# Rows of ordered experts in two blocks of 112 partitions, bounds two less, the second part's rows turned later, the last rows weighted by two engines

## The chip, the core and the metric

The kernel runs on one core of a Trainium2 chip. The metric is the device time of one launch in microseconds (us). The kernel before takes 459.31 us, the median of three runs (458.78 to 460.84). The profile is one execution of the same program under the hardware profiler; its span is 464.4 us. The engines are TensorE (PE; its weight loads are listed apart as PEld), VectorE (DVE), ScalarE (ACT), GpSimd (POOL) and SyncE (SP), which issues most transfers. Sixteen DMA engines move the data.

## The reference

A gated linear attention is followed by a mixture of experts in two levels. Only the second half is touched here; it reads the attention's output as `x` of 3072 rows by 384.

```python
g_idx = argmax(x @ w_group, axis=1)            # 4 groups
g_w   = softmax(x @ w_group)[rows, g_idx]
out = zeros((3072, 384))
for g in range(4):
    mask_g = g_idx == g
    xg = x[mask_g]
    e_idx = argmax(xg @ w_expert[g], axis=1)   # 4 experts in each group
    e_w   = softmax(xg @ w_expert[g])[rows, e_idx]
    for e in range(4):
        mask_e = e_idx == e
        h  = maximum(xg[mask_e] @ w1[g, e], 0) # 384 -> 1024
        ye = h @ w2[g, e]                      # 1024 -> 384
        out[rows of g, e] = (g_w * e_w)[:, None] * ye
```

So each of 3072 rows goes to one of 16 experts. With these inputs the experts get between 158 and 213 rows. One expert's two matrices are 3 MB.

## The kernel before

The attention sends each finished row, with its weight and its row number (386 floats in all), by an indirect transfer into the slots of its expert in DRAM (`slots_d`). Then 17 jobs follow. Jobs 0 and 1 do expert 0: 128 early rows, and 96 more slots. Jobs 2 to 16 do the other 15 experts in order of their number of rows. The order is known only at run time, so a job of rank `r` has a fixed bound `cap(r)` of slots: 220, 218, 214, 212 and so on down to 178. A slot without a row holds zeros and a row number that is out of bounds, so that it is not written. Rows beyond the bound would be done by a loop at the end, once for each 128 of them.

```python
def cap(r):
    return CAP - 4 - 3 * r + r % 2            # CAP = 224
...
jobs = [dict(e=e, parts=[(0, EARLY)], rows=early_rows[:, e:e + 1, :]) for e in range(FIXED)]
jobs += [dict(e=e, parts=[(0, CAP - EARLY)]) for e in range(FIXED)]
jobs += [dict(r=r, parts=[(0, cap(r) // 2), (cap(r) // 2, cap(r) // 2)]) for r in range(NS)]
```

A job's rows are fetched into two parts of equal size. Part 0 holds the even slots and part 1 the odd slots, so that a partition takes two neighbouring slots of 1544 B each, 3088 B in one piece:

```python
def fetch_rows(job):
    e, (_, n), k = expert(job), job["parts"][0], len(job["parts"])
    job["rows"] = mp.tile([P, 2, XW], F32, name="xg", bufs=5)
    c0 = EARLY if k == 1 else 0
    nc.sync.dma_start(
        out=job["rows"][0:n, 0:k, :],
        in_=slots_d.rearrange("(e n) w -> e n w", e=NE)[ds(e, 1), c0:c0 + k * n, :].rearrange(
            "o (p t) w -> (o p) t w", t=k))
```

For each job, `columns` turns the rows (`xt`, by TensorE), `hidden` makes `hT` (line 628 on TensorE, line 630 on ScalarE), `result` makes `yT` (lines 643 and 645), and `deliver` turns it back, weights it, and scatters the rows to the output. `deliver` for a job runs inside the next job's `hidden`.

```python
def deliver(yT, c0, n, weight, dst):
    zy = bank()                                            # one of 7 PSUM banks
    for dc in range(DC):
        nc.tensor.transpose(zy[0:n, dc * P:(dc + 1) * P], yT[:, dc, c0:c0 + n], ident)
    yo = mp.tile([P, DM], F32, name="yo", bufs=3)
    nc.vector.tensor_scalar(out=yo[0:n], in0=zy[0:n, 0:DM], scalar1=weight, ...)   # L657
    nc.gpsimd.indirect_dma_start(out=out_by.popleft(), out_offset=dst, in_=yo[0:n], ...)  # L659
...
for j, job in enumerate(jobs):
    if 1 < j < len(jobs) - AHEAD:
        fetch_rows(jobs[j + AHEAD])                        # AHEAD = 3
    e, (_, n), k = job["e"], job["parts"][0], len(job["parts"])
    w1, w2 = weights[max(0, j - 1)]
    dst = mp.tile([P, 2], I32, name="dst")                 # two buffers
    nc.vector.tensor_copy(out=dst[0:n, 0:k], in_=job["rows"][0:n, :k, DM + 1])     # L805
    hT = hidden(w1, xt, k * n, {2: [deliver_last], 4: [last_gates] if j == 0 else []})
    if j == 0:
        order, excess, ceiling = by_number()
        fetch_rows(jobs[1])
        load_weights(1, expert(jobs[2]))
        for ahead in jobs[2:AHEAD + 2]:
            fetch_rows(ahead)
    elif j + 2 < len(jobs):
        load_weights(j + 1, expert(jobs[j + 2]))           # two buffers of w1, two of w2
    if j + 1 < len(jobs):
        xt = columns(jobs[j + 1], *([nc.scalar.copy] if j == 0 else []))   # turns, L613
    ...
    last = (job, result(w2, hT, k * n), dst)
deliver_last()
```

[...]

Of the kernel before, what the change touches and what calls it, by code (L numbers as in the profile page):

```python
# [16 lines left out]
ALU = mybir.AluOpType  # L17
AF = mybir.ActivationFunctionType
# [16 lines left out]
def gla_then_hierarchical_moe(  # L35
# [32 lines left out]
    nc = tc.nc  # L68
# [10 lines left out]
    DM = H * D  # L79
# [8 lines left out]
    CAP = 224  # L88
    FIXED, EARLY, EARLY_T = 1, P, (B - 1) * NC
    NS = NE - FIXED  # L90

    def cap(r):
        return CAP - 4 - 3 * r + r % 2

    NX = -(-(N - CAP) // P)
    XW = DM + 2
# [8 lines left out]
    def bank():  # L105
        return pp.tile([P, 512], F32, name="bank")
# [58 lines left out]
    def load_weights(i, e):  # L165
        w1 = wp.tile([P, DC, F], F32, name="w1")
        w2 = wp.tile([P, FC, DM], F32, name="w2")
        nc.sync.dma_start(out=w1.rearrange("p c f -> p (c f)"),
                          in_=w1_d[ds(e, 1)].rearrange("o p f -> p (o f)"))
        nc.sync.dma_start(out=w2.rearrange("p c f -> p (c f)"),  # L170
                          in_=w2_d[ds(e, 1)].rearrange("o p f -> p (o f)"))
        weights[i] = (w1, w2)
# [20 lines left out]
    with ExitStack() as gla:  # L193
# [17 lines left out]
        for u in range(3):  # L211
            w = units[u][2] * (2 * P + A1) + 1
            for p in range(HP):
                if not spare or width + w > DC * F:
                    k = len(spare)
# [333 lines left out]
        for n in range(LAST):  # L549
# [47 lines left out]
            if n == 2:  # L597
                nc.sync.dma_start(
                    out=slots_d.rearrange("(e n) w -> e n w", e=NE)[:, 0:CAP, :].rearrange(
                        "e (p t) w -> p e (t w)", t=2),  # L600
                    in_=blank[0:CAP // 2, None, :].to_broadcast([CAP // 2, NE, 2 * XW]))
# [7 lines left out]
    def turned(xg, xt, n, c0, copy=nc.vector.tensor_copy):  # L609

        z = bank()
        for dc in range(DC):
            nc.tensor.transpose(z[:, dc * P:dc * P + n], xg[0:n, dc * P:(dc + 1) * P],  # L613
                                ident[0:n, 0:n])
        copy(  # L615
            out=xt[:, :, c0:c0 + n],
            in_=z[:, 0:DM].rearrange("p (c t) -> p c t", c=DC)[:, :, 0:n])

    def hidden(w1, xt, n, between={}):
        hT = mp.tile([P, FC, CAP], F32, name="hT")  # L620
        for f0 in range(0, FC, 2):
            for fn in between.get(f0, ()):
                fn()
            z = bank()
            for k in range(2):
                f = f0 + k
                for dc in range(DC):
                    nc.tensor.matmul(z[:, k * n:(k + 1) * n], lhsT=w1[:, dc, f * P:(f + 1) * P],  # L628
                                     rhs=xt[:, dc, 0:n], start=(dc == 0), stop=(dc == DC - 1))
            nc.scalar.activation(out=hT[:, f0:f0 + 2, 0:n],  # L630
                                 in_=z[:, 0:2 * n].rearrange("p (f t) -> p f t", f=2), func=AF.Relu)
        return hT

    def result(w2, hT, n):

        yT = mp.tile([P, DC, CAP], F32, name="yT")
        for d0 in range(0, DC, 2):
            k = min(2, DC - d0)
            z = bank()
            for i in range(k):  # L640
                dc = d0 + i
                for f in range(FC):
                    nc.tensor.matmul(z[:, i * n:(i + 1) * n], lhsT=w2[:, f, dc * P:(dc + 1) * P],  # L643
                                     rhs=hT[:, f, 0:n], start=(f == 0), stop=(f == FC - 1))
            nc.scalar.copy(out=yT[:, d0:d0 + k, 0:n],  # L645
                           in_=z[:, 0:k * n].rearrange("p (c t) -> p c t", c=k))
        return yT

    out_by = deque(dram_disjoint_views(out, 2 * NE + 1))

    def deliver(yT, c0, n, weight, dst):

        zy = bank()
        for dc in range(DC):
            nc.tensor.transpose(zy[0:n, dc * P:(dc + 1) * P], yT[:, dc, c0:c0 + n], ident)  # L655
        yo = mp.tile([P, DM], F32, name="yo", bufs=3)
        nc.vector.tensor_scalar(out=yo[0:n], in0=zy[0:n, 0:DM], scalar1=weight, scalar2=None,  # L657
                                op0=ALU.mult)
        nc.gpsimd.indirect_dma_start(  # L659
            out=out_by.popleft(), out_offset=bass.IndirectOffsetOnAxis(ap=dst, axis=0),  # L660
            in_=yo[0:n], in_offset=None, bounds_check=N - 1, oob_is_err=False)

    def columns(job, *copies):
        xt = mp.tile([P, DC, CAP], F32, name="xt_e")
        for t, (c0, n) in enumerate(job["parts"]):
            turned(job["rows"][:, t, :], xt, n, c0, *copies[t:t + 1])
        return xt
# [42 lines left out]
    def by_number():  # L710
# [18 lines left out]
        with nc.allow_low_precision("whole numbers below 2**24"):  # L729
# [5 lines left out]
        nc.vector.tensor_copy(out=odd, in_=rank)  # L735
        nc.vector.tensor_scalar(out=odd, in0=odd, scalar1=1, scalar2=None, op0=ALU.bitwise_and)
        nc.vector.tensor_scalar(out=ceil, in0=odd, scalar1=float(cap(0)), scalar2=None, op0=ALU.add)
        nc.vector.scalar_tensor_tensor(out=ceil, in0=rank, scalar=-3.0, in1=ceil,
                                       op0=ALU.mult, op1=ALU.add)
# [3 lines left out]

    jobs = [dict(e=e, parts=[(0, EARLY)], rows=early_rows[:, e:e + 1, :]) for e in range(FIXED)]
    jobs += [dict(e=e, parts=[(0, CAP - EARLY)]) for e in range(FIXED)]
    jobs += [dict(r=r, parts=[(0, cap(r) // 2), (cap(r) // 2, cap(r) // 2)]) for r in range(NS)]

    def expert(job):

        if "e" not in job:  # L750
            r = job["r"]
            job["e"] = nc.values_load(order[0:1, r:r + 1], engines=[ENG.SP], min_val=FIXED,
                                      max_val=NE - 1,
                                      skip_runtime_bounds_check_because="an index of one of NE")
        return job["e"]
# [5 lines that stand above are left out]
        nc.sync.dma_start(  # L761
            out=job["rows"][0:n, 0:k, :],
            in_=slots_d.rearrange("(e n) w -> e n w", e=NE)[ds(e, 1), c0:c0 + k * n, :].rearrange(
                "o (p t) w -> (o p) t w", t=k))

    last = None

    def deliver_last():
        if last is not None:
            job, yT, dst = last  # L770
            for t, (c0, n) in enumerate(job["parts"]):
                deliver(yT, c0, n, job["rows"][0:n, t, DM:DM + 1], dst[0:n, t:t + 1])


    AHEAD = 3
# [11 lines left out]
    xt = columns(jobs[0], nc.scalar.copy)  # L787
# [11 lines left out]
    for j, job in enumerate(jobs):  # L799
        if 1 < j < len(jobs) - AHEAD:  # L800
            fetch_rows(jobs[j + AHEAD])
        e, (_, n), k = job["e"], job["parts"][0], len(job["parts"])
        w1, w2 = weights[max(0, j - 1)]
        dst = mp.tile([P, 2], I32, name="dst")
        nc.vector.tensor_copy(out=dst[0:n, 0:k], in_=job["rows"][0:n, :k, DM + 1])  # L805
        hT = hidden(w1, xt, k * n, {2: [deliver_last], 4: [last_gates] if j == 0 else []})
        if j == 0:
            order, excess, ceiling = by_number()
            fetch_rows(jobs[1])
            load_weights(1, expert(jobs[2]))  # L810
            for ahead in jobs[2:AHEAD + 2]:
                fetch_rows(ahead)
        elif j + 2 < len(jobs):
            load_weights(j + 1, expert(jobs[j + 2]))
        if j + 1 < len(jobs):
            xt = columns(jobs[j + 1], *([nc.scalar.copy] if j == 0 else []))
        if j == 3:
            first, whose, n_more = left_over()
        last = (job, result(w2, hT, k * n), dst)
    deliver_last()  # L820


    n_left = nc.values_load(n_more[0:1, 0:1], min_val=0, max_val=NX,
                            skip_runtime_bounds_check_because="a count of at most NX")
    with tc.For_i(0, n_left) as i:  # L825
# [4 lines left out]
        e = nc.values_load(who[0:1, 0:1], engines=[ENG.SP], min_val=0, max_val=NE - 1,  # L830
                           skip_runtime_bounds_check_because="an index of one of NE")
        load_weights("left", e)
        w1, w2 = weights.pop("left")
# [4 lines left out]
            out=xg[:, 0, :], out_offset=None, in_=slots_d,  # L838
# [4 lines left out]
        xt = mp.tile([P, DC, CAP], F32, name="xt_e")  # L843
        turned(xg[:, 0, :], xt, P, 0)
        hT = hidden(w1, xt, P)
# [64 lines left out]
```

## Time and profile before

| | before |
|---|---|
| median of three runs | 459.31 us |
| span of the profiled execution | 464.4 us |
| TensorE busy | 417.9 us (90%) |
| GpSimd busy | 161.7 us (35%) |
| VectorE busy | 151.2 us (33%) |
| ScalarE busy | 124.4 us (27%) |
| moved by DMA | 94.83 MB |
| line 628 on TensorE (first matrix) | 816 instructions, 139.4 us |
| line 643 on TensorE (second matrix) | 816 instructions, 139.1 us |
| scatters to the output, line 659 | 32 |
| fetches of rows, line 761 | 16 |

In the timeline each row is a start, a duration, an engine, a line of the kernel, an operation with its output and input, and a count of merged instructions; the brackets give the idle time of the engine before it and what ended it. The name after the arrow is inferred; `issue` means that the profile shows nothing that was waited for. A table by stretch of time gives for each engine the busy time and the number of instructions, then the clock granted to TensorE (1.00 is full speed), the mean busy share of the 16 DMA engines, and the bytes moved per second.

### The profile page before, as it was taken

What the parts mean: (1) busy time and instruction counts of PE and PEld (TensorE: products, weight loads), DVE (VectorE), ACT (ScalarE), POOL (GpSimd) and SP (SyncE); (2) the same over time, 40 slices, a digit from 0 to 9 for tenths busy, and PEclk for the clock granted to TensorE, in tenths of its full rate; (3) what the DMA queues carried; (4) which work ended last, traced back from release to release, by engine and by line L of the source; (5) the groups of instructions that cost most, each with busy time, mean ns of one, the idle gap of its engine ahead of it and who ended that gap; (6) DMA issues with size and microseconds to landing.
All of it is one profiled execution on the core that took longest, in us unless ns stands there. A gap on an engine that the chain in (4) does not pass through costs nothing. (4 is left out here: it accounts for less than half of the span.)

```text
span 464.4 us, 8829 instructions
## 1 busy us (share of the span) xinstructions
PE 417.9 (90%) x3538; PEld 396.8 (85%) x3538; DVE 151.2 (33%) x439; ACT 124.4 (27%) x305; POOL 161.7 (35%) x197
## 2 busy tenths in 40 slices
PE   5999999999974999499999689999999999999950
PEld 4888888878854999399999689999999999999950
DVE  6868788878546010026010011001011101101000
ACT  2465765566541111011111102112111111111200
POOL 6877788898744000010312021033011121202130
PEclk9999999999998899799999979999999999999995
DMA  8999988951123717745545825565766656653000
GB/s 260 409 355 376 364 329 298 368 208 44 63 77 117 303 43 261 266 145 227 195 170 166 281 76 201 207 211 192 238 238 211 229 205 217 240 186 145 22 4 20
DMA packets 25265, 94.83 MB, mean 204 GB/s; under 512 B 9860, under 2 KB 10945, under 8 KB 20744
## 3 DMA queue, kind: packets, MB, share of 16 engines
q1 hardware_dynamic: 14424, 84.70, 50.2%
q0 software_dynamic: 10800, 9.56, 6.8%
q8 instruction: 29, 0.48, 0.4%
q14 instruction: 12, 0.10, 0.1%
HBM read 79.17 MB, written 15.22 MB: 203 GB/s over the span
## 5 line engine op out<-in xcount | busy, mean ns | idle before, releaser
L628 PE MATMUL bank<-xt_e,w 128*128 128x128 f32 (+16 forms) x816 | 139.4, 328 | 7.4 <-DMA w<-in_w_dram 6.6
L643 PE MATMUL bank<-hT,w 128*128 128x128 f32 (+16 forms) x816 | 139.1, 332 | 5.8 <-DVE yo L657 5.8
L643 PEld LDWEIGHTS bank<-hT,w 128*128 128x128 f32 x816 | 135.4, 195 | 6.2 <-DVE yo L657 6.0
L628 PEld LDWEIGHTS bank<-xt_e,w 128*128 128x128 f32 x816 | 133.5, 192 | 8.1 <-issue 6.9
L659 POOL DMA_INDIRECT out_dram<-yo,dst x32 | 49.0, 1531 | 257.6 <-DVE yo L657 238.0
L630 ACT ACTIVATE hT<-bank 128x256 f32<-128x256 f32 (+16 forms) x68 | 32.9, 486 | 122.3 <-PE bank L628 116.6
L645 ACT COPY yT<-bank 128x256 f32<-128x256 f32 (+33 forms) x34 | 13.5, 396 | 133.6 <-PE bank L643 133.6
L657 DVE TENSOR_SCALAR yo<-bank,xg 110x384 f32<-110x384 f32 (+15 forms) x31 | 17.7, 611 | 80.2 <-PE bank L655 80.2
L805 DVE CAST dst<-xg 96x1 int32<-96x1 f32 (+15 forms) x16 | 2.6, 165 | 107.0 <-issue 93.3
L282 PE MATMUL bank<-qp,kp 48*128 48x128 f32 x384 | 31.9, 298 | 5.7 <-POOL qp L270 5.6
L615 DVE COPY xt_e<-bank 128x330 f32<-128x330 f32 (+14 forms) x30 | 12.7, 464 | 64.0 <-PE bank L613 64.0
L282 PEld LDWEIGHTS bank<-qp,kp 48*128 48x128 f32 x384 | 24.9, 192 | 9.5 <-POOL qp L270 6.4
L295 POOL TENSOR_SCALAR_AFFINE_SELECT sm<-sm 128x512 f32<-128x512 f32 x43 | 26.4, 635 | 15.1 <-ACT sm L294 15.1
L359 PE MATMUL bank<-sm,v 128*48 128x128 f32 (+1 forms) x384 | 30.7, 283 | 0.8
L378 PE MATMUL bank<-wr,yt 112*128 112x116 f32 x192 | 27.6, 286 | 3.3 <-ACT yt L366 2.9
L378 PEld LDWEIGHTS bank<-wr,yt 112*128 112x128 f32 x192 | 23.2, 191 | 7.3 <-ACT yt L366 6.1
L294 ACT COPY sm<-bank 128x512 f32<-128x512 f32 x43 | 23.3, 590 | 15.8 <-PE bank L282 14.9
L478 POOL DMA_INDIRECT slots_d<-xr,place x24 | 24.1, 1005 | 9.8 <-issue 4.7
L359 PEld LDWEIGHTS bank<-sm,v 128*48 128x48 f32 (+1 forms) x384 | 23.4, 133 | 3.6 <-POOL sm L295 3.0
L268 DVE TENSOR_TENSOR_SCAN cq<-qka,starts 112x387 f32<-112x387 f32 x24 | 23.0, 959 | 2.5
L270 POOL TENSOR_TENSOR qp<-qka,cq 112x384 f32<-112x384 f32 x24 | 21.9, 913 | 3.0 <-DVE cq L268 2.8
L335 ACT ACTIVATE state<-gained,rev 112x48 f32<-112x48 f32 x64 | 16.2, 323 | 25.3 <-DVE gained L327 18.8
(116 smaller groups left out, 336.1 us busy)
## 6 DMA issues: line engine op xcount, KB each, us to landing
w<-in_w_dram SPq DMA_DIRECT2D x32, 1536.0 KB
qka<-in_qka_dram SPq DMA_DIRECT2D x24, 578.0 KB
slots_d<-blank SPq DMA_DIRECT2D x1, 5404.0 KB
v<-in_v_dram SPq DMA_DIRECT2D x3, 1152.0 KB
w<-in_qka_dram SPq DMA_DIRECT2D x4, 578.0 KB
w<-in_qka_dram SPq DMA_DIRECT2D x4, 385.5 KB
w<-in_qka_dram SPq DMA_DIRECT2D x4, 193.0 KB
v<-in_v_dram SPq DMA_DIRECT2D x1, 576.0 KB
```

Source lines behind the costliest of these rows:

```text
L268: nc.vector.tensor_tensor_scan(out=flat(cq), data0=a[:, 0:W], data1=st, initial=1.0, op0=ALU.mult, op1=ALU.min)
L270: nc.gpsimd.tensor_tensor(out=qp, in0=q, in1=cq[:, :, 1:A1], op=ALU.mult)
L282: nc.tensor.matmul(z[i][:, p * P:(p + 1) * P], lhsT=kp[r, p, c, :], rhs=qp[r, p, c, :], start=True, stop=True)
L294: nc.scalar.copy(out=sm[:, i], in_=z[i])
L295: nc.gpsimd.affine_select(out=sm[:, i], in_=sm[:, i], pattern=[[0, HP], [1, P]], compare_op=ALU.is_ge, fill=0.0, base=0, channel_multiplie ...
L359: nc.tensor.matmul(z[o, p * P:(p + 1) * P], lhsT=vs[b][:, bc, h * D:h * D + o.stop - o.start], rhs=sm[:, i, p, :], start=(p == 0 and bc == ...
L378: nc.tensor.matmul(z[:, p * W:(p + 1) * W], lhsT=yt[:, p, :], rhs=wr[:, p, :], start=True, stop=True)
L478: nc.gpsimd.indirect_dma_start(out=slots_by_tile[t], out_offset=bass.IndirectOffsetOnAxis(ap=place[:, c:c + 1], axis=0), in_=x[:, c0 + c, ...
L628: nc.tensor.matmul(z[:, k * n:(k + 1) * n], lhsT=w1[:, dc, f * P:(f + 1) * P], rhs=xt[:, dc, 0:n], start=(dc == 0), stop=(dc == DC - 1))
L630: nc.scalar.activation(out=hT[:, f0:f0 + 2, 0:n], in_=z[:, 0:2 * n].rearrange("p (f t) -> p f t", f=2), func=AF.Relu)
L643: nc.tensor.matmul(z[:, i * n:(i + 1) * n], lhsT=w2[:, f, dc * P:(dc + 1) * P], rhs=hT[:, f, 0:n], start=(f == 0), stop=(f == FC - 1))
L659: nc.gpsimd.indirect_dma_start(out=out_by.popleft(), out_offset=bass.IndirectOffsetOnAxis(ap=dst, axis=0), in_=yo[0:n], in_offset=None, bo ...
```

## The change

Five things change, all in the experts.

1. Rows of an ordered expert are fetched as two blocks: slots 0 to 111 in part 0 and slots 112 to 223 in part 1, 112 partitions for every rank (for the last one 96 partitions, slots 0 to 95 and 96 to 191). A partition now takes two separate pieces of 1544 B. Part 0 uses all of its block; part 1 uses `cap(r) - 112` of it (`cap(r) - 96` for the last). The number of partitions of a fetch and the row count of a scatter are thereby chosen, instead of following from half the bound.
2. The bounds are two less for each rank: 218, 216, 212, down to 176. With these inputs every expert still fits.
3. The rows of job 1, expert 0's second part, are turned after job 0's second matrix, not ahead of it, so that job 0 need not wait for their arrival.
4. In the last job, part 1 (80 rows) is weighted by ScalarE while VectorE weights part 0 (96 rows).
5. The destinations are copied for both parts over the first part's partitions.

```diff
     def cap(r):
-        return CAP - 4 - 3 * r + r % 2
+        return CAP - 6 - 3 * r + r % 2
...
-    def deliver(yT, c0, n, weight, dst):
+    def deliver(yT, c0, n, weight, dst, by_scalar=False):
...
-        nc.vector.tensor_scalar(out=yo[0:n], in0=zy[0:n, 0:DM], scalar1=weight, scalar2=None,
-                                op0=ALU.mult)
+        if by_scalar:
+            nc.scalar.activation(out=yo[0:n], in_=zy[0:n, 0:DM], func=AF.Copy, scale=weight)
+        else:
+            nc.vector.tensor_scalar(out=yo[0:n], in0=zy[0:n, 0:DM], scalar1=weight, scalar2=None,
+                                    op0=ALU.mult)
...
-    jobs += [dict(r=r, parts=[(0, cap(r) // 2), (cap(r) // 2, cap(r) // 2)]) for r in range(NS)]
+
+    for r in range(NS):
+        n = CAP // 2 if r + 1 < NS else 96
+        jobs.append(dict(r=r, parts=[(0, n), (n, cap(r) - n)]))
...
-                "o (p t) w -> (o p) t w", t=k))
+                "o (t p) w -> (o p) t w", t=k))
...
-                deliver(yT, c0, n, job["rows"][0:n, t, DM:DM + 1], dst[0:n, t:t + 1])
+                deliver(yT, c0, n, job["rows"][0:n, t, DM:DM + 1], dst[0:n, t:t + 1],
+                        t == 1 and job is jobs[-1])
...
-        e, (_, n), k = job["e"], job["parts"][0], len(job["parts"])
+        e, parts = job["e"], job["parts"]
+        n = sum(m for _, m in parts)
...
-        nc.vector.tensor_copy(out=dst[0:n, 0:k], in_=job["rows"][0:n, :k, DM + 1])
-        hT = hidden(w1, xt, k * n, {2: [deliver_last], 4: [last_gates] if j == 0 else []})
+        k = parts[0][1]
+        nc.vector.tensor_copy(out=dst[0:k, 0:len(parts)],
+                              in_=job["rows"][0:k, 0:len(parts), DM + 1])
+        hT = hidden(w1, xt, n, {2: [deliver_last], 4: [last_gates] if j == 0 else []})
...
-        if j + 1 < len(jobs):
-            xt = columns(jobs[j + 1], *([nc.scalar.copy] if j == 0 else []))
+        if 0 < j < len(jobs) - 1:
+            xt = columns(jobs[j + 1])
...
-        last = (job, result(w2, hT, k * n), dst)
+        last = (job, result(w2, hT, n), dst)
+        if j == 0:
+            xt = columns(jobs[1], nc.scalar.copy)
```

## The prediction

> **What bounds the kernel now.** I read the page's busy shares first (TensorE 90% of the span), then the table of engine time by stretch to see where the other 10% lies, then the timeline around each hole, and last the DMA share in short stretches. The table by stretch (stretch, length, busy time and count of PE, PEld, DVE, ACT, POOL, then clock, DMA share, GB/s):
>
> ```profile
> 145.00:170.00 25.00, 18.56 (x156) 18.59 (x157) 5.12 (x19) 3.33 (x10) 1.97 (x2) 0.86 0.47 179
> 170.00:189.00 19.00, 18.96 (x107) 18.51 (x106) 1.59 (x4) 2.92 (x7) 0.93 (x1) 1.00 0.55 187
> 189.00:216.00 27.00, 20.42 (x108) 20.15 (x109) 9.08 (x23) 3.00 (x6) 2.01 (x2) 0.87 0.60 215
> 216.00:253.00 37.00, 37.00 (x218) 36.91 (x217) 4.11 (x9) 5.91 (x12) 9.19 (x4) 1.00 0.54 179
> 253.00:280.00 27.00, 21.17 (x112) 20.76 (x111) 2.19 (x6) 2.97 (x7) 3.12 (x2) 0.87 0.54 180
> 280.00:447.00 167.00, 167.00 (x1074) 166.62 (x1073) 19.89 (x47) 27.58 (x60) 28.67 (x20) 1.00 0.55 191
> 447.00:464.40 17.40, 1.08 (x8) 0.64 (x6) 1.14 (x2) 0.31 (x1) 4.11 (x2) 0.62 0.08 16
> ```
>
> From 145 us on the experts run, and TensorE sets the pace: it is full except for one hole in each of three stretches, each with a lower clock, and a tail of 17 us in which it does nothing. The change starts at 145 us; what lies before keeps its instructions. The holes in the timeline (start, duration, engine, line, operation; in brackets the idle time before and its releaser):
>
> ```profile
> 151.44 0.71 PE L613 MATMUL bank<-ident,xg 96*128 96x96 f32 x3 [6.52 <-DMA xg<-slots_d]
> 164.29 12.77 SPq L168 DMA_DIRECT2D w<-in_w_dram  x1
> 195.58 3.98 PE L628 MATMUL bank<-xt_e,w 128*128 128x218 f32 x12 [6.62 <-DMA w<-in_w_dram]
> 267.94 0.17 DVE L805 CAST dst<-xg 104x2 int32<-104x2 f32 x1 [22.66 <-issue]
> 268.72 11.19 PE L643 MATMUL bank<-hT,w 128*128 128x208 f32 x48 [5.83 <-DVE yo L657]
> ```
>
> Hole C (6.5 us): the turns of the second job's rows stand ahead of the first job's second matrix, so both wait for the rows. Hole A (6.6 us): a weight matrix lands late, because its issue took 12.77 us instead of the usual 0.33. Hole B (5.8 us): VectorE sat in its copy of the destinations, so it did not empty the bank that TensorE needed. Why were issue and copy held up? The DMA share in that time, in the same columns:
>
> ```profile
> 166.00:169.00 3.00, 3.00 (x29) 3.00 (x28) 0.17 (x1) 0.32 (x1) 0.00 (x0) 1.00 0.06 26
> 169.00:172.00 3.00, 3.00 (x22) 3.00 (x22) 0.00 (x0) 0.24 (x1) 0.00 (x0) 1.00 0.06 26
> 172.00:175.00 3.00, 3.00 (x19) 2.94 (x18) 0.61 (x1) 0.54 (x1) 0.93 (x1) 1.00 0.06 26
> ```
>
> 0.06 is one sixteenth: a single DMA engine worked, at 26 GB/s, while 1.5 MB of weights waited. What was in flight were fetches of rows into 109 and 107 partitions, both prime. The scatters of the output show the same by their row count (109, 104 and 89 rows):
>
> ```profile
> 219.72 2.32 POOL L659 DMA_INDIRECT out_dram<-yo,dst  x1 [16.55 <-DVE yo L657]
> ...
> 283.28 1.01 POOL L659 DMA_INDIRECT out_dram<-yo,dst  x1 [10.89 <-DVE yo L657]
> ...
> 448.89 2.06 POOL L659 DMA_INDIRECT out_dram<-yo,dst  x1 [11.49 <-DVE yo L657]
> 451.25 2.05 POOL L659 DMA_INDIRECT out_dram<-yo,dst  x1 [0.30 <-issue]
> ```
>
> Prime counts (109, 107, 103, 101, 97, 89) take 2.05 to 2.3 us on GpSimd, counts with many divisors 1.0. The landings follow: the destination copy that reuses a buffer ends its wait 5.9 us after the issue of the second 98-row scatter and 8.3 us after 100 rows, but 14 to 23 us after 97, 101, 107 and 109. In the tail, two scatters of 89 rows (137 KB each) move until 461:
>
> ```profile
> 455.00:456.00 1.00, 0.00 (x0) 0.00 (x0) 0.00 (x0) 0.00 (x0) 0.00 (x0) 0.50 0.15 38
> 459.00:460.00 1.00, 0.00 (x0) 0.00 (x0) 0.00 (x0) 0.00 (x0) 0.00 (x0) 0.50 0.07 28
> 461.00:462.00 1.00, 0.00 (x0) 0.00 (x0) 0.00 (x0) 0.00 (x0) 0.00 (x0) 0.50 0.00 0
> ```
>
> [...] clock 0.50 in 193 to 196 and 0.55 in 196 to 199, 1.00 after.
>
> **The change part by part.**
>
> Rows in two blocks. Every fetch of an ordered expert is 112 partitions of two rows (96 for the last)[...]. It moves a few more bytes (224 rows, 346 KB) in pieces of 1544 B instead of 3088[...]. Scatters become 112 rows[...] and a rest of 106, 104, 100, 98, 94, 92, 88, 86, 82, 80, 76, 74, 70, 68: none prime[...]. Before, two blocks of 106 rows landed 8.3 us after the second issue, which stalled no one.
>
> - Hole A goes: 6.62, and the cold clock after it. Job starts in the timeline are 18.59 us apart at 214 columns and 15.95 at 182, so 0.0825 us per column; at 218 I expect 18.92 and see 195.58 to 215.91 = 20.33, so 1.41 for the clock. Together 8.0.
> - Hole B goes: the job with 208 columns took 252.92 to 279.57 = 26.65 against 18.09 by that slope. 8.6 (5.83 idle, 2.7 clock).
>
> Bounds two less: 2 columns by 0.0825 us by 15 jobs = 2.5 us, all on TensorE's path. No expert's rows exceed the lower bounds: the smallest margin with these inputs is 2 rows, so the loop for leftovers still runs no time.
>
> Second part's rows turned later (hole C). The order of instructions shows the first job's second matrix directly after its hidden layer. It can begin as soon as hT is there: the last two activations run from 147.22 to 147.88 (their wait of 3.3 us, put down to a remote event, I leave as it is). Four of eight chunks can go before that. The remaining 40 matmuls at 0.122 us (24 took 2.92) end near 152.5 instead of 158.4; then three turns (0.5), ScalarE's copy and its hand-offs (0.9, TensorE idle), so the second job starts near 154 instead of 158.4. But the next turns then come at 160, when the rows of the third job, behind 3.1 MB of weights, are only landing (the DMA share falls from 0.95 at 157 to 160 to 0.13 at 161 to 162): I charge 1.6 us. Net 2.8.
>
> The tail. The last two scatters are 96 and 80 rows[...]. Before, from TensorE's last second-matrix result (447.18) to the end are 17.2 us. After: first scatter issued at +1.7, 0.95 long, second at +3.0 to +3.9, data from about +5.9 (2 us after the scatter ends on GpSimd, as now from 453.30 to the second flow at 455), [...]and the 3.7 us that pass now between the last byte (460.7) and the end: 10.0. Gain 7.2. The weighting by ScalarE adds nothing: GpSimd's first scatter occupies 448.89 to 450.95 and VectorE was done at 449.1; with scatters of 0.95 us the second could start 0.7 us after VectorE. I book 0.
>
> Sum: 8.0 + 8.6 + 2.5 + 2.8 + 7.2 = 29.1 us of the profiled 464.4.
>
> **Rivals.** First, the halves: the holes could be filled by another wait. Weights per job are 3.1 MB, rows and scatter 0.7 MB, together 3.8 MB per 17 us = 224 GB/s, where stretches here reach 422; and a weight has about 27 us from the freeing of its buffer to its use. So bandwidth speaks against it. If a hole of 5 us stayed ([...]the third job's rows landing late), the time would be near 438. Second, smaller pieces of 1544 B could slow fetches and the weights beside them[...]. It would cost under 2 us, at the first jobs alone: 432. Third, that holes A and B have another cause (clock or HBM), and only columns, tail and hole C come: 12.5 us, 447. The single engine's share in the trace speaks against it. Fourth, TensorE without pauses could be throttled further; 280 to 447 at a clock of 1.00 speaks against that.
>
> **Range and chances.** Timed runs lie 5 us under the profiled span, so stalls may be a little smaller there: 459.3 - 29.1 = 430.2, and I say 431. All of it: 426. One hole of 5 to 8 us kept: 438. Tail and columns alone (9.7 us) already pass 2%, so faster 0.97, same 0.02, slower 0.01.
>
> **What would show it.** Right: TensorE 100% busy from about 153 to the last result with at most one short wait near 160; no stretch with a DMA share of 0.06; no weight issue over 1 us; GpSimd's scatters of 112 rows at about 1.0 us; the end about 10 us after the last result. Wrong: an idle TensorE over 3 us after 165, a clock below 1.00 there, a destination copy that waits over 15 us after its scatter, or a tail still over 13 us. A start of the leftover loop would add tens of microseconds and overturn everything.

## The result and the profile after

The changed kernel takes 440.25 us (439.74 to 441.57) against 459.37 us before; the ratio is 0.958 (95% interval 0.955 to 0.962). A median counts every launch, while a ratio leaves out those more than 1.5% above the fastest of their kernel. That is 19.1 us saved where 28 were predicted; the time lies above the range's upper end of 438. The span of its profiled execution is 439.5 us.

The table by stretch of the changed kernel, with the same columns as before (stretch, length, busy time and count of PE, PEld, DVE, ACT, POOL, then clock, DMA share, GB/s):

```profile
145.00:170.00 25.00, 19.50 (x144) 19.02 (x144) 2.24 (x8) 2.92 (x9) 0.97 (x1) 0.86 0.70 251
170.00:189.00 19.00, 19.00 (x109) 18.90 (x109) 1.58 (x4) 3.02 (x6) 0.94 (x1) 1.00 0.53 192
189.00:216.00 27.00, 27.00 (x159) 26.82 (x158) 10.21 (x25) 4.55 (x9) 4.48 (x4) 1.00 0.64 225
216.00:253.00 37.00, 37.00 (x224) 36.84 (x223) 4.37 (x11) 6.34 (x13) 3.89 (x4) 1.00 0.59 207
253.00:280.00 27.00, 27.00 (x163) 26.93 (x162) 2.89 (x8) 3.74 (x9) 2.43 (x2) 1.00 0.55 200
280.00:424.00 144.00, 144.00 (x942) 143.61 (x941) 17.57 (x42) 23.83 (x52) 18.96 (x18) 1.00 0.54 197
```

From 170 us on TensorE has no hole and a full clock: A and B are gone. The first stretch still holds 5.5 us of idle TensorE and a clock of 0.86. The timeline of the changed kernel shows where:

```profile
142.93 5.52 PE L643 MATMUL bank<-hT,w 128*128 128x128 f32 x48
149.18 0.44 PE L613 MATMUL bank<-ident,xg 96*128 96x96 f32 x3 [0.73 <-DMA xg<-slots_d]
160.29 1.32 PE L613 MATMUL bank<-ident,xg 112*128 112x112 f32 x6 [4.28 <-DMA xg<-slots_d]
161.41 7.99 PE L643 MATMUL bank<-hT,w 128*128 128x96 f32 x48
178.62 0.33 SPq L168 DMA_DIRECT2D w<-in_w_dram  x1
191.47 0.95 POOL L662 DMA_INDIRECT out_dram<-yo,dst  x1 [17.64 <-DVE yo L660]
192.72 1.57 POOL L662 DMA_INDIRECT out_dram<-yo,dst  x1 [0.30 <-issue]
```

The first job's second matrix now starts at once (142.93), but TensorE stops 4.28 us at 156 for the rows of the third job, and the 48 matmuls after that run cold, that is, at a lower granted clock (0.50 from 160 to 166 us): 7.99 us, where the same 48 took 5.51 before. The weight's issue takes 0.33 us again. The scatter of 112 rows takes GpSimd 0.95 us, that of 106 rows 1.57.

The tail of the changed kernel, from the last scatter on, in the timeline and by stretch:

```profile
430.06 0.91 POOL L662 DMA_INDIRECT out_dram<-yo,dst  x1 [0.30 <-issue]
```

```profile
432.00:433.00 1.00, 0.00 (x0) 0.00 (x0) 0.00 (x0) 0.00 (x0) 0.00 (x0) 0.91 0.04 14
433.00:434.00 1.00, 0.00 (x0) 0.00 (x0) 0.00 (x0) 0.00 (x0) 0.00 (x0) 0.50 0.00 0
435.00:439.50 4.50, 0.00 (x0) 0.00 (x0) 0.00 (x0) 0.00 (x0) 0.00 (x0) 0.50 0.00 0
```

The bytes are out at 432.5, yet the program ends 7.0 us later; before, 3.6 us passed.

### The profile page after: what moved, and what is told of

Same layout as the page of the kernel before. It is cut to its first block, busy times and chain, and to the rows that moved or that the text cites. A ratio compares the mean times of both kernels' runs of the same rounds, so it can differ in the third digit from the quotient of the medians.

```text
span 439.5 us, 8833 instructions
## 1 busy us (share of the span) xinstructions
PE 413.3 (94%) x3538; PEld 391.9 (89%) x3538; DVE 150.5 (34%) x438; ACT 125.5 (29%) x306; POOL 146.3 (33%) x197
## 4 chain that ended last, share of the span: by engine, by line
issue 61%; PE 19%; POOL 14%; DVE 2%; ACT 1%; DMA 1%; SPq 0%; POOLq 0%; DVEq 0%; ACTq 0%
POOL out_dram L662 6%; PE bank L282 4%; PE bank L359 4%; PE bank L378 4%; PE bank L347 3%; POOL qp L270 3%; POOL sm L295 2%; POOL kp L263 2%; PE bank L319 2%; PE bank L628 1%; PE bank L307 1%; DMA w<-in_qka_dram 1%; DVE rev L260 1%; POOL slots_d L478 1%; ACT sm L294 1%
## 5 line engine op out<-in xcount | busy, mean ns | idle before, releaser
L628 PE MATMUL bank<-xt_e,w 128*128 128x128 f32 (+16 forms) x816 | 136.7, 324 | 1.2 <-ACT xt_e L615 1.2
L643 PE MATMUL bank<-hT,w 128*128 128x128 f32 (+16 forms) x816 | 136.8, 329 | 0.0
L643 PEld LDWEIGHTS bank<-hT,w 128*128 128x128 f32 x816 | 133.3, 195 | 0.0
L628 PEld LDWEIGHTS bank<-xt_e,w 128*128 128x128 f32 x816 | 131.1, 190 | 1.6 <-ACT xt_e L615 1.6
L662 POOL DMA_INDIRECT out_dram<-yo,dst x32 | 33.5, 1047 | 253.1 <-DVE yo L660 239.4
L660 DVE TENSOR_SCALAR yo<-bank,xg 112x384 f32<-112x384 f32 (+15 forms) x30 | 17.2, 612 | 146.1 <-PE bank L655 146.1
L645 ACT COPY yT<-bank 128x192 f32<-128x192 f32 (+32 forms) x34 | 13.4, 394 | 130.4 <-PE bank L643 130.4
L615 DVE COPY xt_e<-bank 128x336 f32<-128x336 f32 (+15 forms) x30 | 12.7, 461 | 86.2 <-PE bank L613 86.2
L359 PE MATMUL bank<-sm,v 128*64 128x128 f32 (+1 forms) x384 | 30.6, 280 | 1.0 <-POOL sm L295 0.5
L294 ACT COPY sm<-bank 128x512 f32<-128x512 f32 x43 | 23.3, 588 | 17.2 <-PE bank L282 15.8
L263 POOL TENSOR_TENSOR kp<-qka,rev 112x384 f32<-112x384 f32 x24 | 22.4, 934 | 0.9 <-DVE rev L260 0.8
```

The costliest lines, as they stand in the source:

```text
L263: nc.gpsimd.tensor_tensor(out=kp, in0=k, in1=rev[:, :, 1:A1], op=ALU.mult)
L294: nc.scalar.copy(out=sm[:, i], in_=z[i])
L359: nc.tensor.matmul(z[o, p * P:(p + 1) * P], lhsT=vs[b][:, bc, h * D:h * D + o.stop - o.start], rhs=sm[:, i, p, :], start=(p == 0 and bc == ...
```

## The experiments

**Before, once more (two runs).** The edit is none. The first:

> The kernel before, profiled once more. Theory: the profiled execution of before was 7 us longer than its timed runs, because hole B (5.8 us of idle TensorE and 2.7 of cold clock, 8.6 in all) belongs to that execution and not to most. Then this profile has a span near 457 us, holes C and A as before (6.5 and 6.6 us idle), and no idle TensorE over 1 us near 263. Rival: the profiler itself lengthens before; then the span is again near 464 and hole B is there again, and the change took it away in the timed runs as well.

Its profile has a span of 461.5 us. The second:

> The kernel before, one more profile. Theory: hole A (6 to 7 us idle and cold clock, 8 in all) is in every execution, hole B differs from one to the next, and takes the span with it: the span less hole B's loss is 455.5 to 456.5 us, as it was in the other two profiles (464.4 less 8.6, and 461.5 less 5.4). Rival: the span varies with something else, such as the attention before 137 us; then the span less the loss at hole B lies outside of that.

That one has a span of 455.3 us. What TensorE waited for in each, from the view of waits (us in total, times, longest), first run, then second:

```profile
PE bank L613 <- DMA xg<-slots_d: 6.0, 1, 6.0
PE bank L628 <- DMA w<-in_w_dram: 5.7, 1, 5.7
PE bank L643 <- DVE yo L657: 3.5, 2, 2.4
```

```profile
PE bank L613 <- DMA xg<-slots_d: 5.8, 1, 5.8
PE bank L628 <- DMA w<-in_w_dram: 5.8, 1, 5.8
PE bank L643 <- DVE yo L657: 0.9, 1, 0.9
```

Holes C and A are nearly the same in all three profiles of before (5.7 to 6.6 us each). Hole B is not: 5.8 us of idle in the profile I predicted from, two shorter waits of 3.5 us together in the next, one of 0.9 us in the third. With the cold clock after it, read from the distances of job starts, it cost 8.6, 5.4 and 1.1 us (the wait is not always in the same job: 2.4 us near 263 and 1.1 near 338 in the second profile); less that, the spans are 455.8, 456.1 and 454.2 us. The third is 1.3 us under what I had expected, and its second job starts 1.3 us earlier (156.98 against 158.30): what lies ahead of the experts varies by about that much. Launches of the unchanged kernel lay between 456.1 and 468.2 us. So the theory of the first run missed its numbers (461.5 and not 457, and a wait of 2.4 us where it allowed 1), and holds in kind: the profiled execution was no typical one, and hole B is most of what made it longer than the others. The rival, that the profiler lengthens every execution of before, falls with the third profile.

**Fetches into 112 partitions, nothing else.** Before, with

```diff
         e, (_, n), k = expert(job), job["parts"][0], len(job["parts"])
+        if k == 2:
+            n = CAP // 2
```

in the fetch of rows: 112 partitions of two neighbouring slots, in pieces of 3088 B as before; halves, scatters, bounds and turns unchanged.

> Before, with one edit: every fetch of an ordered expert takes 112 partitions (slots 2p and 2p+1 as before, 3088 B in a piece); parts, scatters, bounds and turns as before. Theory: hole A comes from fetches on one DMA engine alone. Then no weight issue is over 1 us, hole A goes with its clock (8.0 us), hole C and the tail stay (6.5 idle and some 17 us): 451 us. Rival: prime scatters hold the weights up, too; then hole A stays at 4 us or more and the time is 456 to 460.

It takes 451.51 us (450.17 to 454.97) against 459.65 of before beside it, ratio 0.985 (0.975 to 0.995), which is some 7 us. The launches alone do not put the gain clear of 2%; the profile shows what went. By stretch:

```profile
189.00:216.00 27.00, 27.00 (x157) 26.90 (x156) 10.21 (x25) 4.85 (x10) 6.45 (x4) 1.00 0.61 214
253.00:280.00 27.00, 26.88 (x163) 26.57 (x162) 4.26 (x11) 3.92 (x8) 5.14 (x4) 1.00 0.60 213
```

Hole A is gone with its clock (1.00 from 189 to 216 us, where it was 0.87), and no weight issue exceeds 1 us. The third and the fourth job together take 37.7 us, against 46.1, 46.4 and 46.2 in the three profiles of before. The rival falls, since the prime scatters are still there. TensorE has no hole near 263 either, although the scatters still have prime counts and VectorE still waits for them. In the first of these two copies the profile names nothing, in the next it names the scatter:

```profile
253.77 0.17 DVE L807 CAST dst<-xg 104x2 int32<-104x2 f32 x1 [16.96 <-issue]
264.88 0.17 DVE L807 CAST dst<-xg 103x2 int32<-103x2 f32 x1 [9.08 <-DMA out_dram<-yo,dst]
```

A wait of 17 us in the first copy just fits into the slack that TensorE has, one of 22.7 did not. So the partition counts of the fetches are the cause of hole A: 109 and 107 before, at a DMA share of 0.06, and 112 here. Whether the fetches also take part in hole B this one profile can't tell, since one of before had only 0.9 us of it. The wait behind hole B belongs to the scatters: the longest wait of this copy is 17.0 us here, and 22.7 and 19.2 in the first two profiles of before, but 1.4 in that of the changed kernel. The runs still lie 4.8 us apart; that these waits make the spread is likely, but I didn't show it apart.

**Turns back ahead.** The changed kernel with

```diff
-        if 0 < j < len(jobs) - 1:
-            xt = columns(jobs[j + 1])
+        if j + 1 < len(jobs):
+            xt = columns(jobs[j + 1], *([nc.scalar.copy] if j == 0 else []))
...
-        if j == 0:
-            xt = columns(jobs[1], nc.scalar.copy)
```

> The changed kernel with the turns of the second job's rows put back ahead of the first job's second matrix. Theory: turning later gained nothing, because the wait moved to the third job's rows; here the first wait is 6 us again at about 145, the wait for the third job's rows is under 1 us, and the time is 439 to 441.5. Rival, as in the prediction: turning later is worth 2.8 us, and this run takes 443.

It takes 441.80 us (440.67 to 442.02), a little above the theory's window and below the rival's 443; ratio 0.962 (0.954 to 0.970), which overlaps that of the changed kernel. Its timeline:

```profile
149.42 0.71 PE L613 MATMUL bank<-ident,xg 96*128 96x96 f32 x3 [4.33 <-DMA xg<-slots_d]
163.25 0.73 PE L613 MATMUL bank<-ident,xg 112*128 112x112 f32 x6
```

TensorE waits ahead of the first job's second matrix, and then finds the third job's rows there. The second job starts at 157.61 instead of 150.11, 7.5 us later, and yet the third starts at 169.16 instead of 169.23. Turning later moved the wait from the second job's rows to the third's, and what is left of it is at most some 1.5 us.

**Rows first.** The changed kernel with the third job's rows fetched ahead of that job's weights:

```diff
-            load_weights(1, expert(jobs[2]))
-            for ahead in jobs[2:AHEAD + 2]:
+            fetch_rows(jobs[2])
+            load_weights(1, expert(jobs[2]))
+            for ahead in jobs[3:AHEAD + 2]:
```

> The changed kernel with the rows of the third job fetched ahead of that job's two weight matrices, not behind them. Theory: the 4.3 us of idle TensorE at 156 to 160 and the cold clock after it (some 3.3 us) are paid because the rows share the DMA engines with 3.1 MB of weights; then both go, and the time is 433 (432 to 434.5). Rival: the transfers as a whole set the pace there, and the wait moves to the weights: 438 to 440.5.

434.06 us (433.35 to 434.17), ratio 0.944 (0.936 to 0.952).

> The changed kernel with the third job's rows fetched ahead of the weights, repeated beside the others: 434 us, 6 under the changed kernel's 440.3.

434.28 us (434.12 to 434.46), ratio 0.946 (0.939 to 0.952). In the profile of the repeat:

```profile
149.73 0.44 PE L613 MATMUL bank<-ident,xg 96*128 96x96 f32 x3 [0.43 <-DMA xg<-slots_d]
156.39 0.73 PE L613 MATMUL bank<-ident,xg 112*128 112x112 f32 x6
156.95 5.51 PE L643 MATMUL bank<-hT,w 128*128 128x96 f32 x48
```

```profile
145.00:170.00 25.00, 24.08 (x190) 23.68 (x189) 3.66 (x14) 4.50 (x12) 1.90 (x2) 1.00 0.87 307
```

No wait at 156, no cold clock, and the third job starts at 162.31 instead of 169.23. The 3.1 MB of weights arrive in time behind the rows: the rival falls. This beats both kernels, by 6 us and by 25 us.

**Rows first, and turns back ahead.** Both of the last edits together:

> The changed kernel with the third job's rows fetched ahead of the weights, and the second job's rows turned ahead of the first job's second matrix again. Theory: turning later is worth its 6 us only when the next wait is gone too; here TensorE waits some 4 to 6 us again at about 145, the third job starts near 169 and the time is 440 to 441. Rival: with the rows first the earlier turns cost nothing: 434.

441.70 us (441.04 to 442.01), ratio 0.961 (0.955 to 0.968); the third job starts at 169.78. In its timeline:

```profile
149.62 0.71 PE L613 MATMUL bank<-ident,xg 96*128 96x96 f32 x3 [5.71 <-DMA xg<-slots_d]
```

It is a little above the 440 to 441 that I expected. So the later turns and the earlier rows are worth 7.5 us together, and either alone at most about 1.5: the third job waits for whichever comes last.

**Bounds back.** The changed kernel with `CAP - 4` in the bounds:

> The changed kernel with the bounds of before (220, 218, 214 down to 178); the last job's second part is then 82 rows. Theory: two more columns in 15 jobs cost 0.165 us each, 2.5 in all, [...]and GpSimd takes about 1.5 instead of 0.9 us: together 4.5 to 5.5, some 445 us. Rival: only the columns count, 442.8.

446.41 us (446.17 to 447.52), ratio 0.973 (0.966 to 0.980): 6.1 above the changed kernel's 440.3, a little more than expected. Job starts give the columns: 169.23 to 412.06 in the changed kernel, 168.99 to 414.09 here, 2.3 us for 14 jobs. Most of the rest is the tail: from the end of the last scatter on GpSimd to the end of the span are 11.2 us (8.5 in the changed kernel), and GpSimd takes 1.41 us for 82 rows.

**79 instead of 80 rows at the end.** The changed kernel with

```diff
-        jobs.append(dict(r=r, parts=[(0, n), (n, cap(r) - n)]))
+        jobs.append(dict(r=r, parts=[(0, n), (n, cap(r) - n if r + 1 < NS else 79)]))
```

> The changed kernel with 79 rows instead of 80 in the last job's second part (79 is prime; its expert has 158 rows for 175 slots, so nothing is left out). One column less by 96 matmuls saves 0.1 us. Theory: the row count alone puts the last scatter on one engine: 79 rows of 1536 B (121 KB) at 26 GB/s are 4.7 us, GpSimd takes about 2 us for it instead of 0.9, and the end comes 2 to 4.5 us later than in the changed kernel: 442 to 444.5. Rival: the tail's gain came from the smaller blocks and not from the count; then within 0.5 us of the changed kernel.

446.81 us (446.15 to 447.31), ratio 0.974 (0.970 to 0.977), against 440.36 of the changed kernel on the same chip: 6.5 us for one row less, more than I had expected. The timeline and the tail by stretch of this kernel:

```profile
429.42 1.92 POOL L662 DMA_INDIRECT out_dram<-yo,dst  x1 [0.30 <-issue]
```

```profile
432.00:434.00 2.00, 0.00 (x0) 0.00 (x0) 0.00 (x0) 0.00 (x0) 0.00 (x0) 0.55 0.18 12
434.00:436.00 2.00, 0.00 (x0) 0.00 (x0) 0.00 (x0) 0.00 (x0) 0.00 (x0) 0.50 0.05 18
436.00:438.00 2.00, 0.00 (x0) 0.00 (x0) 0.00 (x0) 0.00 (x0) 0.00 (x0) 0.50 0.05 20
```

From 434 to 437.6 rows move at 18 to 20 GB/s and a share of 0.05, near the one sixteenth of a single engine, as expected; in the changed kernel the last two scatters moved at a share of 0.45 and 123 GB/s from 430 to 432. The term I missed lies ahead of it: from 432 to 434 the engines are busy (0.18) and move almost nothing (12 GB/s). The DMA view of the last 17.6 us here, and of the last 12.5 us of the changed kernel, shows what kind of packets:

```profile
DMA packets 498, 0.27 MB, mean 15 GB/s; under 512 B 443, under 2 KB 443, under 8 KB 496
```

```profile
DMA packets 98, 0.27 MB, mean 21 GB/s; under 512 B 39, under 2 KB 39, under 8 KB 96
```

The scatter of 79 rows brings some 400 packets of under 512 B more than that of 80 (443 against 39). What these packets are, no view shows.

**Both parts by VectorE.** The changed kernel without the last argument of `deliver`:

> The changed kernel with both parts of the last job weighted by VectorE. Theory: the second engine gives nothing, because GpSimd is busy with the first scatter until the second product is there: within 0.4 us of the changed kernel. Rival: the second scatter starts later by VectorE's 0.6 us, and the time is 0.6 higher.

440.35 us (440.10 to 441.67) against 440.36: nothing. Its timeline shows GpSimd in the way, as expected: VectorE ends at 427.94, the second scatter starts at 428.90, 0.3 us after the first.

**No loop at the end.** The changed kernel without the loop for leftover rows. Rows beyond the bounds would be left out.

> The changed kernel without the loop for leftover rows at the end (left out: rows beyond the bounds, of which there are none with these inputs). Theory: the tail fell by 4.9 us and not 7.2 because, with the last bytes at 432.3, the engines' own way past the loop[...] ends last at 439.5; without it the end comes 3.7 to 4.5 us after the last byte and the time is 2 to 3.5 us lower than the changed kernel's, some 437. Rival: the 7 us from the last byte to the end belong to the closing of any program: within 0.5 us of the changed kernel.

438.38 us (437.63 to 439.32), ratio 0.955 (0.952 to 0.958), 2.0 under 440.36. The bytes are out at about 433.3 and the span ends at 437.6, 4.3 us later instead of 7.0. At the very end SyncE waits for TensorE's sequencer; the line of that wait in the profile of before, of the changed kernel (with its wait for the scatter ahead of it) and of this one:

```profile
SPq L906 <- PEq L906: 2.3, 2, 1.8
```

```profile
SPq L837 <- DMA out_dram<-yo,dst: 12.7, 1, 12.7
SPq L918 <- PEq L918: 5.6, 2, 5.0
```

```profile
SPq L894 <- PEq L894: 3.2, 2, 2.7
```

The changed kernel waits 5.0 us there, before 1.8. So the loop costs 2.0 us at the end although it runs no time, which is the lower edge of what I expected. The way there is another than I supposed, though. I had the engines pass the loop beside the last transfer and come out of it last, because the bytes were early. But SyncE waits for the scatter at the loop's own line (L837), and the time from the last byte to the end does not depend on when that byte lands: it is 6.8 to 7.0 us in all nine profiles that have both the change and the loop, also with 79 and with 82 rows, where the bytes are out 5 us later. It is 3.6 us in the three profiles of before and in the one with fetches alone. So it follows the last byte with a length that belongs to the program. Why that length grew by 3.4 us with the change, where the loop was the same, stays open. It is not the fetch into 112 partitions (3.6 us with it alone), and not the later turns, the bounds or ScalarE's weighting (6.9 us without each).

**The changed kernel again.**

> The changed kernel itself, once more, to compare the next runs with on the same chip. Theory: [...]its runs lie within 2 us of each other, where those of before lie up to 12 apart; 440 us. Rival: the spread of before is the chip's, and these runs spread likewise.

440.36 us (439.82 to 441.76), ratio 0.959 (0.956 to 0.962). Its runs lie within 1.9 us of each other. The seven of before beside it lie 9.2 apart, but 2.5 without the one of 467.0, so this pair alone would not decide. All launches together do: of 63 of before, 14 took over 463 us, which is 7 above the shortest; of 40 of the changed kernel and its variants, none lay more than 2.1 us above the shortest of its kernel. The spread belongs to the kernel before, not to the chip.

## Why the prediction was wrong

The direction held, and so did the mechanism of hole A, of the bounds and of the bytes in the tail. Three terms of the sum were too large, and the base was wrong. For the size I take the third profile of before (455.3) against that of the changed kernel (439.5).

| step | predicted | measured | from |
|---|---|---|---|
| hole A and its clock | 8.0 | 8.5 | third and fourth job together 46.2 us (168.53 to 214.72), with fetches alone 37.7 |
| hole B and its clock | 8.6 | 1.1 | one wait of 0.9 us in the third profile; 5.4 and 8.6 in the others |
| bounds two less | 2.5 | 2.3 | job starts with fetches alone against turns back, less 0.4 us lost in one job; 2.3 for 14 jobs with the bounds put back |
| turns later | 2.8 | -0.7 | third job at 169.23 instead of 168.53 |
| tail | 7.2 | 4.6 | 12.3 us after the last second matrix instead of 16.9 |
| ScalarE's weighting | 0 | 0 | VectorE alone |

The measured terms sum to the 15.8 us between these two profiles. The rest up to 19.1 is in the executions: the median of before lies 1.8 us above the run of this profile (457.56), and the median after lies 1.3 below its profiled run (441.57). If all of the 1.8 us is hole B, it costs some 3 us in a launch of median length; that is an estimate.

**Hole B: the step that failed most.** I took 8.6 us from one execution as if every execution had it. The hint was in my own working: timed runs lay 5 us under the profiled span (7.3 in truth, for a span is some 2.2 us shorter than the time of its launch, which was 466.6), and I wrote that stalls may be a little smaller there, and then subtracted the whole 29.1 from the timed 459.3. A hole behind a wait of 12 to 23 us for a late scatter hangs on little (17.0 us cost nothing with fetches alone, 22.7 cost 5.8); its size in one trace is no mean. It was bad luck that the trace came from a long execution; to take its hole as every execution's was the error.

**Turns later: the charge was too small.** I booked a gain of 4.4 and charged 1.6 us for the third job's rows. The rows landed about when I said (160.2), but TensorE asked for them at 156.0, not at 160. The 3.3 us for which ScalarE waited in the hidden layer, which I "left as it is", were in that one execution alone of all that were profiled, so that everything before the wait came earlier and the wait took it all back: 4.28 us of idle, 2.5 of cold clock on the second matrix, and 0.6 on the turns. I had counted the cold clock for holes A and B and forgotten it here.

**The tail: right in the bytes, wrong in the end.** The last bytes were out even sooner than predicted (5.3 us after the last second matrix instead of an estimated 6.4), but the time from the last byte to the end, which I carried over as 3.7 us, is no constant across programs: it is 7.0 after the change. That took back 3.4 us of the gain.

**Two slips in the sums, both small.** In hole A, 215.91 is the start of the weight loads of the next job; its matmuls start at 216.09, so the clock cost 1.6 us and not 1.41. In hole C, only 4 of the 48 matmuls of the second matrix can go before the last two activations end, so 44 remain and not 40, 0.5 us more.

**What was right.** The fetches into 109 and 107 partitions were the cause of hole A, and 112 partitions remove it, at about the predicted size (8.5 us against 8.0). A share of 0.06 is what one busy engine of sixteen gives; how many engines any other count of partitions or rows gets was my assumption, and no view shows it. Bandwidth was no new limit: from 170 to 424 us TensorE was busy throughout, at 192 to 225 GB/s. The pieces of 1544 B cost nothing that can be seen: in the first loads the three fetches land after a median of 10.9 us with turns back (1544 B), and after 10.8 with fetches alone (3088 B); over all sixteen fetches the medians are 7.2 and 7.3. No throttling appeared in 250 us of unbroken work (a clock of 1.00 in every stretch from 170 to 424 us). Of the marks I had set, the single wait near 160 and the end near 10 us were the two that showed the errors.

## What to carry to other kernels

Look at the partition count of each transfer and at the row count of each scatter: here fetches into 109 and 107 partitions moved 26 GB/s at a DMA share of 0.06 while 1.5 MB of weights waited, 112 partitions took the wait away, and a last scatter of 79 rows instead of 80 cost 6.5 us. When a wait is removed, look at what is asked for next and when it lands, because two fetches behind the same weights must both be moved; and charge the cold clock after a hole that is left (2.5 us on the second matrix after the 4.28 us here). Size a hole from several executions, above all when timed runs disagree with the profiled span.

## What the runs showed of the hardware

- The time for a scatter did not follow its size: with 80 rows in the last one the kernel is 6.5 us faster than with 79. GpSimd's time for the last scatter was 0.91 us with 80 rows, 1.41 with 82 and 1.92 with 79, and the packets of under 512 B in the tail come in the same order: 39, 235 and 443. The packets I had not expected. In the profile of before the scatters of 109, 107, 103, 101, 97 and 89 rows took GpSimd 2.05 to 2.32 us each, those of other counts 0.93 to 1.56.
- The end of a program follows its last byte with a length of its own: 3.6 us before, 6.8 to 7.0 with the change and the same loop passed over, 4.3 without the loop. SyncE's last wait for TensorE's sequencer goes with it: 1.8, 5.0 and 2.7 us.
- A late scatter can stop TensorE through two other engines (destination copy, VectorE, PSUM bank), by an amount that changes from one execution to the next: 0.9, 3.5 and 5.8 us of idle in three profiles.
